# Strassen's scheme for seven of nine channel groups of a fused attention, expert and FFN kernel

## The chip, the cores and the metric

One core of a Trainium2 chip runs the whole program. The metric is device time in microseconds (us) of one launch; lower is better. Engines: TensorE (PE; its weight loads are listed as PEld), VectorE (DVE), ScalarE (ACT), GpSimd (POOL) and SyncE (SP), whose queue issues most DMAs.

## The reference

```python
attn = softmax(q @ mean_pool8(k).T / 8) @ mean_pool8(v)      # 8 x 8 heads, 576 tokens, 64 wide
x = attn as [4608 tokens, 512]
e = argmax of 8 gate logits (or the previous token's expert, if a local gate says so)
x = softmax(logits)[e] * (relu(x @ w1[e]) @ w2[e])           # 512 -> 1024 -> 512
xn = (x - mean) / sqrt(var + 1e-6) * g_ln
out = x + relu(xn @ w_ch1) @ w_ch2                           # 512 -> 2048 -> 512
```

The change is in the last line, the channel FFN. All data are float32; the kernel makes each float32 product from float16 halves: `hi*hi + hi*lo + lo*hi`, three matmuls that add up in one PSUM bank.

## The kernel before

There are three stages, and every engine follows an order written out by hand.

The attention stage works on 36 tiles of 128 tokens. Routing then sorts the tokens by expert into 39 blocks of 128 rows (`NF = 39`).

The expert stage is the loop `for k in range(NF + 1)`. Block `k` takes 48 matmuls with 512 columns (`moe1`, `moe2`, two halves of 12 each). When the expert changes, new weights are loaded into `f1` and `f2` and split into float16 halves in `s1` and `s2` (`splits1`, `splits2`, line 540). The channel weights come in as 64-bit words and are converted by `conv_slot` and `conv_b2` in the same loop.

The channel FFN works on 9 groups of 512 tokens. `ln(j)` normalises a tile, splits it and has a DMA transpose (line 945, on SP's queue) write it to `xnT`. A *unit* is one of 16 slices of 128 hidden channels of one group: `ffn1(u)` is 12 matmuls of 512 columns into one bank of `ps_f`, ScalarE and VectorE take ReLU and both halves out of it (lines 968 and 969), and `ffn2(u)`, two units later (`LAG`), is 12 matmuls into the four banks of `ps_a`, which hold the group's 512 tokens over 16 units. `ffn2_out` adds the residual, and GpSimd scatters the rows to `out` (line 986).

`mix(k, n)` puts units into the expert loop at `RATE = 1.15` a block from block `FIRST = 8` on; the rest follow when the loop is over, and `ffn2_last` orders the last seven so that tiles finish one after the other. All of PSUM is in use: two banks each for `ps_m` and `ps_f`, four for `ps_a`.

`hs`, `xn` and the like are float32 work tiles; `tick` moves generators (`chains`) on by small steps, so that the small vector work of one tile lies between the matmuls of others.

## Time and profile before

| | |
|---|---|
| median of 3 runs | 1373.8 us (1373.62 to 1373.91) |
| the profiled execution: its own time | 1379.85 us |
| its span on the core | 1377.9 us, mean granted clock 0.986 |
| attention, routing and the first expert blocks | 0 to about 291 us |
| experts with channel units between them | 291 to 811 us |
| channel units alone | 811 to 1371 us |

The rows below are of the profiled execution. A matmul's listed time contains the pipeline behind it, so the time that one takes in a stream is read from the starts of two groups. A bracket at the end of a row is the idle time of the engine before it, and what ended that.

### The profile page before, as it was taken

What the parts mean: (1) busy time and instruction counts of PE and PEld (TensorE: products, weight loads), DVE (VectorE), ACT (ScalarE), POOL (GpSimd) and SP (SyncE); (2) the same over time, 40 slices, a digit from 0 to 9 for tenths busy, and PEclk for the clock granted to TensorE, in tenths of its full rate; (3) what the DMA queues carried; (4) which work ended last, traced back from release to release, by engine and by line L of the source; (5) the groups of instructions that cost most, each with busy time, mean ns of one, the idle gap of its engine ahead of it and who ended that gap; (6) DMA issues with size and microseconds to landing.
All of it is one profiled execution on the core that took longest, in us unless ns stands there. A gap on an engine that the chain in (4) does not pass through costs nothing. (4 is left out here: it accounts for less than half of the span.)

```text
span 1377.9 us, 20409 instructions
## 1 busy us (share of the span) xinstructions
PE 1319.3 (96%) x6512; PEld 662.7 (48%) x6512; DVE 555.0 (40%) x1387; ACT 447.7 (32%) x943; POOL 329.0 (24%) x374
## 2 busy tenths in 40 slices
PE   6999789789999999999999999999999999999998
PEld 5999534334444444444444434444444444444443
DVE  7777884555664243343254531221212222122211
ACT  5888424444443232333143431121211212121110
POOL 3667253343332112321111220110201101020101
PEclk9999989999999999999999999999999999999999
DMA  9997377887995575676476750120201102021000
GB/s 306 296 298 238 138 236 160 146 179 181 216 212 111 93 147 147 132 150 156 90 190 154 190 153 0 39 54 9 68 17 54 39 31 54 8 70 23 31 0 31
DMA packets 213274, 166.85 MB, mean 121 GB/s; under 512 B 163550, under 2 KB 171998, under 8 KB 213152
## 3 DMA queue, kind: packets, MB, share of 16 engines
q1 hardware_dynamic: 199424, 119.32, 36.0%
q0 software_dynamic: 9120, 29.30, 6.9%
q10 hardware_dynamic: 4608, 16.78, 4.9%
q8 instruction: 54, 0.88, 0.3%
q14 instruction: 68, 0.56, 0.2%
HBM read 216.30 MB, written 29.28 MB: 178 GB/s over the span
## 5 line engine op out<-in xcount | busy, mean ns | idle before, releaser
L959 PE MATMUL f_ps<-xnT,c_sb 128*128 128x512 f16 x1728 | 395.6, 379 | 0.0
L978 PE MATMUL a<-c_sb,hf 128*128 128x512 f16 x1680 | 385.6, 379 | 0.0
L969 DVE SCALAR_TENSOR_TENSOR hf<-f_ps,hf 128x512 f16<-128x512 f32 x140 | 96.6, 690 | 436.1 <-ACT hf L968 418.4
L959 PEld LDWEIGHTS <-c_sb 128*128 128x128 f16 x1728 | 169.1, 98 | 203.9
L978 PEld LDWEIGHTS <-hf 128*128 128x128 f16 x1680 | 164.4, 98 | 198.2
L623 PE MATMUL y_ps<-s,hT 128*128 128x512 f16 x936 | 220.4, 386 | 14.7 <-DMA hT<-hs 11.8
L610 PE MATMUL h_ps<-s,xT 128*128 128x512 f16 x936 | 216.9, 382 | 8.5 <-DVE hs L615 6.9
L968 ACT ACTIVATE hf<-f_ps 128x512 f16<-128x512 f32 x140 | 83.4, 596 | 412.6 <-PE f_ps L959 412.6
L623 PEld LDWEIGHTS <-hT 128*128 128x128 f16 x936 | 92.5, 99 | 130.3 <-DMA hT<-hs 13.8
L610 PEld LDWEIGHTS <-xT 128*128 128x128 f16 x936 | 92.2, 98 | 120.7 <-issue 12.8
L986 POOL DMA_INDIRECT out_dram<-yt,ti x36 | 35.4, 984 | 355.9 <-DVE yt L985 312.5
L614 ACT ACTIVATE hs<-h_ps 128x512 f16<-128x512 f32 x78 | 46.5, 597 | 224.7 <-PE h_ps L610 205.9
L615 DVE SCALAR_TENSOR_TENSOR hs<-h_ps,hs 128x512 f16<-128x512 f32 x78 | 53.8, 690 | 160.0 <-ACT hs L614 116.5
L631 POOL DMA_INDIRECT y_d<-yr,sidx x39 | 41.5, 1064 | 213.2 <-ACTq L1067 92.6
L540 DVE SCALAR_TENSOR_TENSOR s<-f,s 128x1024 f16<-128x1024 f32 x53 | 63.8, 1242 | 19.4 <-ACT s L535 18.5
L303 ACT ACTIVATE p<-s,nm 128x72 f32<-128x72 f32 x288 | 65.8, 338 | 8.1 <-DVE nm L289 7.9
L931 POOL TENSOR_TENSOR rs<-rs,mhalf 128x1 f32<-128x1 f32 x36 | 20.8, 577 | 179.3 <-DVE rs L930 179.3
L942 POOL TENSOR_TENSOR xns<-xn,xns 128x512 f16<-128x512 f32 x36 | 42.2, 1173 | 89.1 <-issue 42.4
L279 PE MATMUL s<-kb,qt 128*128 128x144 f32 (+1 forms) x320 | 45.4, 297 | 14.0 <-ACT kb L203 13.6
L535 ACT ACTIVATE s<-f 128x1024 f16<-128x1024 f32 x56 | 55.7, 1047 | 0.0
L337 PE MATMUL o<-v,pt 128*128 128x148 f32 (+1 forms) x320 | 51.8, 298 | 3.5 <-DVE r L356 3.1
L940 ACT ACTIVATE xn<-yt,rs 128x512 f32<-128x512 f32 x36 | 29.3, 814 | 79.3 <-DVE rs L934 72.7
(198 smaller groups left out, 1032.9 us busy)
## 6 DMA issues: line engine op xcount, KB each, us to landing
f<-in_w_dram SPq DMA_DIRECT2D x288, 512.0 KB
xrow_d<-xr SPq DMA_DIRECT2D x36, 260.5 KB
yt<-y_d SPq DMA_DIRECT2D x36, 256.5 KB
kt<-in_kT_dram SPq DMA_DIRECT2D x16, 576.0 KB
qt<-in_qT_dram SPq DMA_DIRECT2D x18, 512.0 KB
vt<-in_vP_dram SPq DMA_DIRECT2D x16, 512.0 KB
c_sb<-in_c_dram ACTq DMA_DIRECT2D x16, 512.0 KB
shared<-in_c_dram ACTq DMA_DIRECT2D x8, 512.0 KB
```

The lines of the kernel that those rows point to most:

```text
L303: nc.scalar.activation(out=p32[:, h, :], in_=s[:, h // 4, NK * (h % 4):NK * (h % 4) + NK], func=AF.Exp, bias=nm[:, h:h + 1],)
L337: nc.tensor.matmul(out=o[c][lo:hi, 2 * VC * e:2 * VC * (e + 1)], lhsT=pt[:, 2 * c + e, lo:hi], rhs=vb[:, 4 * c + 2 * e:4 * c + 2 * e + 2, ...
L535: A.activation(out=hi, in_=src, func=AF.Copy, scale=SW)
L540: V.scalar_tensor_tensor(out=lo[:, 0:v], in0=src[:, 0:v], scalar=SW, in1=hi[:, 0:v], op0=ALU.mult, op1=ALU.subtract)
L610: nc.tensor.matmul(out=ps, lhsT=xT[:, x, c], rhs=s1[:, w, c, 512 * half:512 * half + 512], start=(n == 0), stop=(n == 11))
L614: A.activation(out=hs[:, 0], in_=ps, func=AF.Relu)
L615: V.scalar_tensor_tensor(out=hs[:, 1], in0=ps, scalar=0.0, in1=hs[:, 0], op0=ALU.max, op1=ALU.subtract)
L623: nc.tensor.matmul(out=ps, lhsT=hT[:, f // 4, x, f % 4], rhs=s2[:, w, f], start=(f == 0 and x + w == 0), stop=(f == 7 and x == 1),)
L959: nc.tensor.matmul(out=ps, lhsT=c1_sb[:, w, c, 128 * f:128 * f + 128], rhs=xT[:, x, c], start=(n == 0), stop=(n == 11))
L968: A.activation(out=hf[:, 0], in_=ps, func=AF.Relu)
L969: V.scalar_tensor_tensor(out=hf[:, 1], in0=ps, scalar=0.0, in1=hf[:, 0], op0=ALU.max, op1=ALU.subtract)
L978: nc.tensor.matmul(out=acc_t[t], lhsT=hf_t[u][:, x, 128 * t:128 * t + 128], rhs=c2_sb[:, w, f], start=(f == 0 and n == 0), stop=(f == NC2 ...
```

## The change

The first two groups (`NPL = 2`, 32 units) stay as they were, but at `RATE = 0.87` and with the last five held back (`HOLD`) until the expert loop is over. The other seven groups use the Winograd form of Strassen's scheme: tokens, model width and hidden width are halved, and seven products of half-size blocks take the place of eight, in both layers. The matmuls of these groups have 256 columns instead of 512. For one group, layer 1 is 8 steps (`l1_step`) of 7 products of 6 matmuls; layer 2 is 112 pieces (2 token halves, 8 slices, 7 products) of 3 matmuls, which `fill` puts between and behind them.

The scheme's 15 sums of each layer: four of the inputs, per group (`prep`, both halves of each tile pair written to `xs`, then `xpose` has four DMA transposes of 128 x 1792 float16 write `xnT`); four of the weights, once (`sums_of`, in the expert loop after the conversions, three steps at each `mix`; they go to DRAM and come back by `load_comb` into the buffers of the expert weights and into places of the channel weights that are no longer used); seven of the products (in `l1_step` between PSUM and float32 tiles for layer 1; in `evac` for layer 2). The seven hidden combinations are split again into halves (`post_a`, `post_b`, `post_c`).

```diff
--- before.py
+++ after.py
...
-SX, SW, SN, SC1, SC2 = 2.0 ** 7, 2.0 ** 5, 2.0 ** 3, 2.0 ** 4, 2.0 ** 5
+SX, SW, SN, SC1, SC2 = 2.0 ** 7, 2.0 ** 5, 2.0, 2.0 ** 4, 2.0 ** 5
...
+    c1c_d = dram.tile([4, 128, 2, 2, DC // 2], F16, name="c1c_d")
+    c2c_d = dram.tile([4, 128, 2, NCV // 2, DM // 2], F16, name="c2c_d")
...
-    LASTU = 7
-    hf2 = [None]
-    RATE = 1.15
+    RATE = 0.87
...
+    def ftile(u):
+        return (u % NC2 + (NC2 // 2 if u // NC2 == NPL - 1 else 0)) % NC2
+
     def ffn1(u):
-        g, f = divmod(u, DC // 128)
+        g, f = u // NC2, ftile(u)
         assert all(4 * (f // 4) + i in done for i in range(4))
...
+    NPL = 2
+    NU = NPL * NC2
+    HOLD = 5
...
-                load_f1(k, c, 512 * half)
+                if k < NF - 1:
+                    load_f1(k, c, 512 * half)
...
+    hole1 = c1_sb[:, :, 0:2, DC // 2:DC]
+    hole2 = c2_sb[:, :, NC2 // 2:NC2, DM // 2:DM]
...
+    S_w = [hole1, w1c(f1h, 0), w1c(f1h, 1), w1c(f2h, 0)]
+    T_w = [hole2, w2c(f2h, 1), w2c(s1h, 0), w2c(s1h, 1)]
+
+    def load_comb(t, d, i):
+        for x in range(2):
+            nc.sync.dma_start(out=t[:, x], in_=d[i, :, x])
...
+    def sums_of(q, h):
+        tA, tB = shared[:, 0:512].bitcast(F32), shared[:, 512:1024].bitcast(F32)
+        outs = [cw2[:, 0:512].bitcast(F16), cw2[:, 512:1024].bitcast(F16), ct2.bitcast(F16)]
...
+        def out(t):
+            o = outs[n[0] % 3].rearrange("p (x f) -> p x f", x=2)
+            A.copy(out=o[:, 0], in_=t)
+            yield 0
+            G.tensor_tensor(out=o[:, 1], in0=t, in1=o[:, 0], op=ALU.subtract)
+            i = n[0]
+            n[0] += 1
+            for _ in range(2):
+                yield 0
+            src = o if q == 0 else o.rearrange("p x (c d) -> p x c d", c=2)
+            nc.sync.dma_start(out=dst[i], in_=src)
...
+            tt(ta, a21[:, 0], a22[:, 0], ALU.add)
+            yield 0
+            tt(tb, a21[:, 1], a22[:, 1], ALU.add)
+            yield 0
+            tt(ta, ta, tb, ALU.add)
+            yield from out(tA)
+            tt(tb, ta, a11[:, 0], ALU.subtract)
+            yield 0
+            tt(tb, tb, a11[:, 1], ALU.subtract)
...
+    SUMS = 3
...
-        if k >= FIRST and nu[0] < min(int(RATE * (k - FIRST) + n), NC2 * groups[0]):
+        if k >= FIRST and nu[0] < min(int(RATE * (k - FIRST) + n), NC2 * groups[0], NU - HOLD):
...
+        for _ in range(SUMS):
+            if ncv[0] > len(jobs):
+                next(sums, None)
...
+    def xpose(g):
+        for s in range(2):
+            xs = xs_t.pop((g, s))
+            for x in range(2):
+                nc.sync.dma_start_transpose(out=xnT[:, x, :, 128 * s:128 * s + 128], in_=xs[:, x].rearrange("p o t -> p (o t)"))
...
+        T1, T2, T3, T4 = (tmpT[:, n] for n in range(4))
+        xs = pl_t["pp"].tile([128, 2, 7, HW_], F16, tag="xs", name="xs")
+        xs_t[g, s] = xs
+        a12 = yl[0][:, 0:DM].rearrange("p (n t) -> p n t", n=2)
+        V.tensor_tensor(out=T1, in0=b1, in1=a1, op=ALU.subtract)
+        nc.gpsimd.tensor_tensor(out=T3, in0=b2, in1=b1, op=ALU.subtract)
+        V.tensor_tensor(out=T2, in0=b2, in1=T1, op=ALU.subtract)
+        V.tensor_tensor(out=T4, in0=a2, in1=T2, op=ALU.subtract)
+        A.copy(out=xs[:, 0, 0:2], in_=a12)
+        A.copy(out=xs[:, 0, 2], in_=b2)
+        yield 0
+        A.copy(out=xs[:, 0, 3:7], in_=tmpT)
+        V.tensor_tensor(out=xs[:, 1, 0:2], in0=a12, in1=xs[:, 0, 0:2], op=ALU.subtract)
+        V.tensor_tensor(out=xs[:, 1, 2], in0=b2, in1=xs[:, 0, 2], op=ALU.subtract)
+        if g > NPL:
+            yl_load(g + s, 1 - s)
+        nc.gpsimd.tensor_tensor(out=xs[:, 1, 3:7], in0=tmpT, in1=xs[:, 0, 3:7], op=ALU.subtract)
...
+        if k == NF - 1:
+            for _ in sums:
+                pass
+            load_comb(S_w[1], c1c_d, 1)
+            load_comb(S_w[2], c1c_d, 2)
...
-    while nu[0] < NU:
-        if nu[0] % 2:
-            norm_next(NB)
-        else:
-            load_next(NB + 2)
+    mo.close()
+    pp = pl_t["pp"] = ctx.enter_context(tc.tile_pool(name="pp", bufs=2, side="right", reuse_waits="tile"))
+    load_comb(S_w[0], c1c_d, 0)
+    load_comb(T_w[2], c2c_d, 2)
+    load_comb(T_w[3], c2c_d, 3)
+    load_comb(T_w[0], c2c_d, 0)
+
+    run(lumps, 1)
+    while nu[0] < NU + LAG:
         unit()
         tick(99)
-    ffn2_last()
+        if lumps:
+            run(lumps, 2)
+            if not lumps:
+                xpose(NPL)
+    stats_in(bsel.rearrange("p a b -> p (a b)"))
+    tis = [[take(bsel.rearrange("p a b -> p (a b)"), 1).bitcast(U32) for _ in range(2)] for _ in range(2)]
+    yl_load(NPL + 1, 0)
+    yl_load(NPL + 1, 1)
+    while outq:
+        outq.pop(0)()
...
+    def l1(ps, lhs, i, op, first):
+        n = 0
+        for w, x in TERMS:
+            for k in range(2):
+                nc.tensor.matmul(
+                    out=ps, lhsT=lhs(w, k, i), rhs=xnT[:, x, 2 * op + k], start=(first and n == 0), stop=(n == 5), skip_group_check=True,
+                )
+                n += 1
...
+    L2 = (
+        (0, 0, 0, raw2(NI, 0)), (1, 0, 1, raw2(0, 0)), (4, 1, 0, com2(1)), (5, 1, 1, com2(2)),
+        (3, 2, 0, com2(0)), (6, 2, 1, raw2(0, 1)), (2, 3, 0, com2(3)),
+    )
...
+                        for m, (x, w) in enumerate(TERMS):
+                            nc.tensor.matmul(
+                                out=l2["acc"][b][:, HW_ * o:HW_ * o + HW_], lhsT=h[:, x, op], rhs=rhs(w, i),
+                                start=(i == 0 and o == 0 and m == 0), stop=(i == NI - 1 and m == 2), skip_group_check=True,
+                            )
...
+        A.activation(out=t, in_=P1, func=AF.Copy, scale=SC)
+        yield add(a1, P1, a1)
+        yield add(a1, P2, a1)
+        yield add(U2, P6, t)
+        yield add(U3, P7, U2)
+        yield add(b2, P5, b2)
+        G.tensor_tensor(out=b2, in0=b2, in1=U3, op=ALU.add)
+        yield add(t, P5, U2)
+        yield add(a2, P3, a2)
+        G.tensor_tensor(out=a2, in0=a2, in1=t, op=ALU.add)
+        yield add(b1, P4, b1)
+        G.tensor_tensor(out=b1, in0=b1, in1=U3, op=ALU.add)
...
+        V.tensor_tensor(out=st[:, 0], in0=c22, in1=raw[:, 2], op=ALU.add)
+        V.tensor_tensor(out=st[:, 1], in0=raw[:, 0], in1=st[:, 0], op=ALU.subtract)
+        V.tensor_tensor(out=st[:, 3], in0=raw[:, 1], in1=st[:, 1], op=ALU.add)
...
+    def post_c(fast=False):
+        if pend[0] is None:
+            return
+        raw, st = pend[0][0], pend[0][2]
+        for s in range(2):
+            hi(s, 3, 4, st)
+            if fast and s == 0:
+                low(V, 0, 3, 4, st)
+        for s in range(2):
+            low(V, s, 0, 3, raw)
+        for s in range(fast, 2):
+            low(nc.gpsimd, s, 3, 4, st)
+        pend[0] = None
+
...
+        l1(a, A11, i, 0, True)
+        post_a()
+        A.copy(out=s1, in_=a)
+        run(eq, 3)
+        l1(b, A12, i, 1, True)
+        post_b()
+        l1(c, S1, i, 3, True)
+        V.tensor_tensor(out=raw[:, 1], in0=b, in1=s1, op=ALU.add)
+        l1(a, S2, i, 4, False)
+        A.copy(out=U2, in_=a)
+        run(eq, 3)
+        post_c()
+        if outq:
+            outq.pop(0)()
+        fill(gaps[0])
+        l1(a, S3, i, 5, False)
+        A.copy(out=U3, in_=a)
+        V.tensor_tensor(out=c22, in0=c, in1=U3, op=ALU.add)
+        fill(gaps[1])
+        run(eq, 3)
+        l1(a, A22, i, 6, False)
+        A.activation(out=raw[:, 0], in_=a, func=AF.Relu)
+        run(lumps, 2 if g == NPL else 1)
+        fill(gaps[2])
+        l1(c, S4, i, 2, False)
+        V.tensor_tensor(out=raw[:, 2], in0=c, in1=U2, op=ALU.add)
+        A.activation(out=raw[:, 1:3], in_=raw[:, 1:3], func=AF.Relu)
+        V.tensor_scalar(out=c22, in0=c22, scalar1=0.0, scalar2=None, op0=ALU.max)
+        V.tensor_tensor(out=st[:, 2], in0=c22, in1=raw[:, 0], op=ALU.subtract)
+        run(eq, 2)
+        pend[0] = (raw, c22, st, [], (g, i))
...
+    for g in range(NPL, NG):
+        last = g + 1 == NG
+        for i in range(NI):
+            n = g > NPL or i > 1
+            l1_step(g, i, ((4, 3, 0) if i < NI - 1 else (2, 1, 0)) if n else (0, 0, 0))
+        post_a()
+        post_b()
+        post_c(True)
+        run(lumps, -1)
+        if not last:
+            xpose(g + 1)
+        if g + 2 < NG:
+            lumps += [prep(g + 2, 0), prep(g + 2, 1)]
+        fill(4)
+        for n in range(8 if not last else 10):
+            fill(7)
+            run(eq, -1)
+            if n in (2, 4):
+                outq.pop(0)()
+            if n > 1 and g + 2 < NG:
+                run(lumps, 1)
...
```

## Rows read from the trace of the kernel before

**Rows 1.** The page: busy time of each engine; a group (count, busy, mean ns).

```profile
PE 1319.3 (96%) x6512; PEld 662.7 (48%) x6512; DVE 555.0 (40%) x1387; ACT 447.7 (32%) x943; POOL 329.0 (24%) x374
...
L969 DVE SCALAR_TENSOR_TENSOR hf<-f_ps,hf 128x512 f16<-128x512 f32 x140 | 96.6, 690 | 436.1 <-ACT hf L968 418.4
```

**Rows 2.** Windows: us, busy (instructions) of PE, PEld, DVE, ACT, POOL, clock, DMA.

```profile
300.00:400.00 100.00, 96.57 (x448) 43.59 (x446) 64.18 (x132) 47.56 (x77) 35.51 (x38) 1.00 0.87 203
...
801.00:811.60 10.60, 7.69 (x27) 2.90 (x26) 5.33 (x7) 3.82 (x5) 4.78 (x4) 0.84 0.85 239
...
1100.00:1200.00 100.00, 100.00 (x465) 45.37 (x464) 21.53 (x48) 17.08 (x27) 10.84 (x12) 1.00 0.12 32
```

**Rows 3.** Timeline of TensorE, FFN alone: start us, us, engine, line, shapes.

```profile
1055.08 2.75 PE L959 MATMUL f_ps<-xnT,c_sb 128*128 128x512 f16 x12
...
1060.26 2.75 PE L959 MATMUL f_ps<-xnT,c_sb 128*128 128x512 f16 x12
```

**Rows 4.** Timeline of TensorE, routing: narrower matmuls with weights of their own.

```profile
158.62 0.28 PE L681 MATMUL cps<-oh,shared 128*128 128x288 f16 x1 [0.55 <-DVE oh L675]
...
158.75 0.28 PE L682 MATMUL cps<-oh,shared 128*128 128x288 f16 x1
...
158.87 0.38 PE L153 MATMUL tps<-c_sb,shared 128*128 128x512 f16 x1
...
168.37 5.77 PEld L752 LDWEIGHTS <-c_sb 128*128 128x128 f16 x36 [1.68 <-DVE c_sb L743]
```

**Rows 5.** Windows of line 959: busy (count) up to 811.4 us.

```profile
0.00:811.40 811.40, 101.70 (x444) 43.44 (x444) 0.98 0.73 182
```

**Rows 6.** Timeline of TensorE at the end of the expert stage.

```profile
806.30 0.38 PE L623 MATMUL y_ps<-s,hT 128*128 128x512 f16 x1 [1.86 <-ACT s L535]
...
807.57 4.22 PE L623 MATMUL y_ps<-s,hT 128*128 128x512 f16 x11 [0.88 <-DVE s L540]
```

**Rows 7.** Timeline of the conversion stage: the longer wait of TensorE.

```profile
396.02 2.75 PE L610 MATMUL h_ps<-s,xT 128*128 128x512 f16 x12 [1.81 <-DVE hs L615]
```

**Rows 8.** Groups, 300 to 400 us: count, busy us, mean ns, idle before.

```profile
L133 POOL TENSOR_TENSOR c_sb<-ct,c_sb 128x512 f16<-128x512 f32 x9 | 10.5, 1164 | 19.6 <-ACTq L1078 13.2 <-ACT c_sb L132 4.4 <-ACTq L1067 1.9
...
L582 DVE SCALAR_TENSOR_TENSOR xs<-xg,xs 128x512 f16<-128x512 f32 x6 | 7.8, 1301 | 9.2 <-ACT xs L581 7.8 <-DMA hT<-hs 1.4
```

**Rows 9.** The same groups, 500 to 600 us.

```profile
L582 DVE SCALAR_TENSOR_TENSOR xs<-xg,xs 128x512 f16<-128x512 f32 x7 | 4.8, 691 | 7.2 <-ACT xs L581 7.0 <-DVEq L1067 0.3
```

**Rows 10.** Timeline: single instructions of VectorE, ScalarE and GpSimd.

```profile
163.06 0.46 DVE L727 TENSOR_TENSOR c_sb<-c_sb,oh 128x288 f32<-128x288 f32 x1
...
159.62 0.40 ACT L687 COPY tot<-cps 128x288 f32<-128x288 f32 x1 [5.13 <-DVE shared L686]
...
1057.79 1.16 POOL L942 TENSOR_TENSOR xns<-xn,xns 128x512 f16<-128x512 f32 x1 [2.12 <-issue]
...
1057.87 0.60 ACT L968 ACTIVATE hf<-f_ps 128x512 f16<-128x512 f32 x1 [0.21 <-PE f_ps L959]
```

**Rows 11.** Timeline: VectorE and GpSimd at the same time, routing.

```profile
168.48 2.14 POOL L544 TENSOR_TENSOR s<-ptmp,s 128x512 f16<-128x512 f32 x1 [2.23 <-ACT s L535]
...
169.51 1.13 DVE L746 TENSOR_TENSOR bend<-c_sb 128x8 f32<-128x8 f32 x1
```

**Rows 12.** Timeline: one DMA transpose issued with all queues empty.

```profile
1255.79 1.23 SPq L945 DMA_TRANSPOSE xnT<-xns  x1
```

**Rows 13.** Windows: us, clock, DMA share, GB/s: that transpose, then weight loads.

```profile
1257.25:1257.50 0.25, 1.00 1.13 218
...
1258.25:1258.50 0.25, 1.00 0.11 19
...
198.00:198.25 0.25, 1.00 1.07 393
```

**Rows 14.** Timeline of the last output: matmul, evacuation, scatter.

```profile
1368.47 2.75 PE L978 MATMUL a<-c_sb,hT 128*128 128x512 f16 x12
...
1373.79 0.97 POOL L986 DMA_INDIRECT out_dram<-yt,ti  x1 [5.13 <-issue]
```

More of the change, by code (lines that the diff above doesn't have):

```diff
@@ L25 @@
 DC = 4 * DM
+NCV = DC // 128
 NT = T // 128
@@ L979, in ffn2_mm @@
                 out=acc_t[t], lhsT=hf_t[u][:, x, 128 * t:128 * t + 128], rhs=c2_sb[:, w, f],
-                start=(f == 0 and n == 0), stop=(f == NC2 - 1 and n == 2),
+                start=(n0 == 0 and n == 0), stop=(n0 == NC2 - 1 and n == 2),
             )
@@ L1086, in tile_attention_moe_ffn, with all_sums @@
+    def all_sums():
+        for r in range(2):
+            for c in range(2):
+                yield from sums_of(0, (r, c))
+        for h in range(4):
+            yield from sums_of(1, h)
+    sums = all_sums()
+    SUMS = 3
     pexp(0)
@@ L1109, in mix, with stats_in @@
             conv_b2()
+        for _ in range(SUMS):
+            if ncv[0] > len(jobs):
+                next(sums, None)
+    NG = NT // 4
+    NI = NC2 // 2
+    HW_ = DM // 2
+    xnT = s2f[:, 0:7168].rearrange("p (x o t) -> p x o t", x=2, t=256)
+    snap = s2f[:, 7168:8192].bitcast(F32).rearrange("p (n t) -> p n t", n=2)
+    tmpT = shared.bitcast(F32).rearrange("p (n t) -> p n t", n=4)
+    stat = {}
+    def stats_in(buf):
+        used[0] = 0
+        stat.update(half=take(buf, 1), st=take(buf, 2, 6), mv=take(buf, 2, 2), rs=take(buf, 2, 2))
+        V.memset(stat["half"], -0.5)
@@ L1111, in tile_attention_moe_ffn, with run @@
+    lumps, eq = [], []
+    def run(q, n):
+        while q and n:
+            if next(q[0], None) is None:
+                q.pop(0)
+            else:
+                n -= 1
+    PRE = NF - 5
+    pre = []
     AHEAD = 4
@@ L1170, in tile_attention_moe_ffn @@
             load_next(k)
+        if not pre and nl[0] == 4 * NPL and stored[0] >= 4 and k >= last_block(4 * NPL + 3) + 2:
+            yl_load(NPL, 0)
+            yl_load(NPL, 1)
+            pre.append(k)
+        elif pre and k >= PRE:
+            if k == PRE:
+                stats_in(wq.tile([128, DM], F32, tag="xn", name="xn"))
+                lumps.extend((prep(NPL, 0), prep(NPL, 1)))
+            for _ in range(2):
+                if len(pre) <= 8:
+                    next(lumps[len(pre) > 4])
+                    pre.append(k)
         if k == FIRST - 1:
@@ new lines, in tile_attention_moe_ffn, with fill, evac, add @@
+    l2g = l2_steps()
+    def fill(n):
+        for _ in range(n):
+            if next(l2g, None) is None:
+                return
+    def evac(acc, yr, ti):
+        G = nc.gpsimd
+        P1, P2, P6, P7, P5, P3, P4 = (acc[b][:, HW_ * o:HW_ * o + HW_] for _, b, o, _ in L2)
+        ya, yb = yr
+        t = tq.tile([128, HW_], F32, tag="et", name="et")
+        U2 = tq.tile([128, HW_], F32, tag="eu2", name="eu2")
+        U3 = tq.tile([128, HW_], F32, tag="eu3", name="eu3")
+        def add(out, p, x):
+            return V.scalar_tensor_tensor(out=out, in0=p, scalar=SC, in1=x, op0=ALU.mult, op1=ALU.add)
+        a1, a2, b1, b2 = (y[:, HW_ * d:HW_ * d + HW_] for y in yr for d in range(2))
+        A.activation(out=t, in_=P1, func=AF.Copy, scale=SC)
[10 more added lines that the diff above has]
+        G.tensor_tensor(out=b1, in0=b1, in1=U3, op=ALU.add)
+        for n in range(2):
+            V.tensor_copy(out=ti[n], in_=yr[n][:, DM:YROW])
+        outq.extend(lambda n=n: G.indirect_dma_start(
+            out=out, out_offset=bass.IndirectOffsetOnAxis(ap=ti[n], axis=0), in_=yr[n][:, 0:DM], in_offset=None,
+        ) for n in range(2))
+        yield 0
@@ new lines, in l1_step @@
+    def l1_step(g, i, gaps):
+        a, b, c = bank(), bank(), bank()
+        raw = tq.tile([128, 3, 256], F32, tag="raw", name="raw", bufs=2)
+        c22 = tq.tile([128, 256], F32, tag="c22", name="c22")
+        st = tq.tile([128, 4, 256], F32, tag="st", name="st")
+        U2 = tq.tile([128, 256], F32, tag="u2", name="u2", bufs=2)
+        s1, U3 = snap[:, 0], snap[:, 1]
+        l1(a, A11, i, 0, True)
[29 more added lines that the diff above has]
+        pend[0] = (raw, c22, st, [], (g, i))
@@ new lines, in tile_attention_moe_ffn @@
+    lumps += [prep(NPL + 1, 0), prep(NPL + 1, 1)]
+    for g in range(NPL, NG):
+        last = g + 1 == NG
+        for i in range(NI):
+            n = g > NPL or i > 1
[16 more added lines that the diff above has]
+                run(lumps, 1)
@@ L1185, in words @@
+    run(eq, -1)
+    while outq:
+        outq.pop(0)()
 def words(w):
```

201 lines of the change are left out of this document (168 added, 33 removed).

## The prediction

> **What bounds the kernel now.** I read the page first, then windows by stage, then TensorE's timeline. On the page TensorE is busy in 96% of the span, no other engine in more than 40% [rows 1]. A busy TensorE need not be a full one, so the windows come next: where only channel units run, the granted clock is 1.00, its upper level of 2.4 GHz, and VectorE and ScalarE are busy in a fifth of the time [rows 2]. The timeline there shows that TensorE streams without a hole: a unit's 24 matmuls of 512 columns start 5.18 us after those of the unit before, 215.8 ns each, where 512 columns at 2.4 GHz are 213.3 ns, so some 2.5 ns lie between two [rows 3]. The channel FFN is 144 units, 746 us of the 1378; 37 of them lie in the expert loop (444 matmuls of line 959 by 12) [rows 5]. TensorE sets the time, through the number of columns that it streams, and the change cuts just that.
>
> **The matmuls.** A group before is 16 units x 24 = 384 matmuls of 512 columns, 82.9 us. After it is 8 x 42 + 112 x 3 = 672 of 256 columns. What does one of 256 columns take, each with 128 columns of weights of its own? The stage with 512 cannot show whether the weight load still hides. The nearest rows are two matmuls of 288 columns with different weights: they start 0.13 us apart, and the next follows 0.12 us later; 288 columns are 120 ns [rows 4]. So the load hides at 120 ns. I take 106.7 + 2.5 = 109.2 ns: 672 x 109.2 = 73.4 us, 9.5 us less a group, **66.5 us** for seven. The lower bound of the gap is nothing (71.7 us a group, 78 us gained in all). The other bound is the run of 86 columns, where 36 weight loads take 5.77 us, 162 ns each [rows 4]; there both operands step over 36 elements, here every run is contiguous, so I stand by the 288-column row.
> The Trainium skill speaks against this: "TensorE: Matmul & The Clock Gate", section "Back-to-back issue gap", gives 81 ns for a matmul of 128 columns in a stream with weight loads where the columns alone take 56. By that surcharge of 25 ns, 672 x 7 matmuls would lose 118 us and the change would end slower, at 1458. The 288-column rows show no such surcharge.
>
> **What the expert loop gains and loses.** Ten units fewer run in it; their work comes later or shrinks, and that is in the sum above. Added are the weight sums: 8 calls of 9 VectorE additions of 512 columns (0.69 us, as line 582 takes when GpSimd leaves it alone [rows 9]), 4 ScalarE copies (0.60) and 4 GpSimd subtractions (1.16) [rows 10], spread at three steps a `mix`, twelve of 136 steps a block, from about block 17 to 28. That is 4.4 us of VectorE and 3.3 us of GpSimd a block of some 15 us. The conversions that end there cost as much per block: between 300 and 400 us VectorE was busy 64%, GpSimd 36% [rows 2], nine of GpSimd's subtractions among it [rows 8], and TensorE lost two waits on VectorE, the longer 1.8 us [rows 7]. So **+3 us**, between 0 and 10. SP's queue gets 32 stores that wait for GpSimd's subtraction, and behind them stand the transposes of `hs`; issued two steps after the subtraction, they should find it done.
> At the end of the loop the profile loses about 4.5 us to the last expert's weight splits: 1.86 and 0.88 us of waits [rows 6], and a lower clock (0.84 in these 10.6 us [rows 2]), under which 11 matmuls took 4.22 us instead of 2.5. After the change no unit covers the last two blocks, since the 27 allowed units are used up at block 37; but the normalisations, on which VectorE waited there, are gone too. **0**, from -5 to +5. `load_comb` puts 2 MB on SP's queue in front of the last block's transposes and 6 MB in all behind it; at 393 GB/s [rows 13] 2 MB take 5.3 us, the last six MB some 16 us, under 31 us of plain units (60 + 84 matmuls). `xpose` for the first Strassen group stands behind them.
>
> **The transposes.** Before, 128 x 1024 is issued in 1.23 us [rows 12]; its data move at about 210 GB/s and are through 2.5 us after the start of the issue [rows 13], 1.3 of these moving. Now four of 128 x 1792 can start only when a group's layer 1 has read `xnT`, and the next group's layer 1 needs them all. By size each takes 1.3 x 1.75 = 2.3 us, four with the first's 1.2 us of issue 10.4 us. The cover is 60 pieces of layer 2, 60 x 3 x 109.2 ns = 19.7 us. Cost 0; at half that rate it would still be 19.6 us.
>
> **Entering the Strassen stage.** In the first two steps of the first group there is no layer 2 to fill in. The products share one bank, and each must be read before the next adds to it: TensorE's result reaches ScalarE 0.2 us after its last column (12 matmuls from 1055.08 on stream until 1057.67 [rows 3], ScalarE starts at 1057.87 [rows 10]), a copy of 256 columns takes about 0.37 us (0.40 for 288 [rows 10]). Two or three such gaps a step are some 1.5 us, 3 us for two steps; the first work tiles lie where the old outputs are still being scattered, another 3. **+6 us**, 3 to 12.
>
> **The steady steps.** A step is 42 + 21 matmuls, 6.9 us. VectorE's part: seven operations of 256 columns (0.43 us, between 0.46 for 288 [rows 10] and 0.69 for 512), two of 384 (0.56), one maximum: 4.5 us. GpSimd: two subtractions of 512 columns, 2.3 us. ScalarE: five reads of 0.37 to 0.60 and four copies, 4.3 us. Each fits alone. But VectorE and GpSimd block each other: at 168.48 a GpSimd subtraction that alone takes 1.16 takes 2.14 us beside VectorE, and the tiny VectorE operation after it 1.13 us, to the moment GpSimd ends [rows 11]; line 582, with two inputs in SBUF, took 1301 ns beside the conversions [rows 8] and 691 later [rows 9]. Operations with one input in PSUM show little of the kind: line 969 has a mean of 690 ns over all 140 [rows 1].
> Counted by group, within the eight steps (492 matmuls, 53.7 us): VectorE's operations with both inputs in SBUF are 8 x 2.84 + 2.4 for a `prep` = 25.1 us, GpSimd's 18.6 + 2.9 + 1.9 for an `evac` = 23.4. Together 48.5 us of 53.7, and in a plain step they take turns: VectorE until about 4.2 us into the step, GpSimd from there to 6.5. It fits, with little room. Where `prep` subtracts 1024 columns on GpSimd (2.3 us), VectorE comes late to `c22`, which TensorE needs before the last product; about 1 us of slack is there. I take 1.5 us a group, **+10.5 us**; the bounds are 0 and, if the two engines never overlapped at all (44.2 + 23.4 = 67.6 us), 13.9 x 7 = 97 us.
> The Trainium skill says the same of this pair: "SBUF — State Buffer", "Who interferes with whom": an operation with two SBUF inputs and a GpSimd one that reads SBUF exclude each other for a whole instruction. By that rule the 48.5 us hold; it is the rule that speaks against this change.
>
> **The end of each group.** After the last product the chain is: 0.2, add 0.43, ReLU of 512 columns 0.60, three additions 1.3, copy 0.60, subtractions 0.69 and 0.56, with some 0.3 us of hand-overs and the second ReLU's two operations beside it about 5.0 us, until layer 2 may use the eighth slice. Eleven pieces and two matmuls stand before, 3.8 us. TensorE waits 1.2 us, and about 0.5 us more where the second token half takes over the banks that `evac` still reads: 1.7 x 7 = **+12 us**, 0 to 25.
>
> **The last output.** Now the last stream ends at 1371.06, and the span 6.85 us later, with the scatter issued at 1373.79 [rows 14]. After: three VectorE additions follow the last product, a GpSimd addition (about 0.6), and two scatters, issued one after the other (0.97 us). **+1.5 us**, 0 to 4.
>
> **Sum.** -66.5 + 3 + 0 + 6 + 10.5 + 12 + 1.5 = -33.5 us. The profiled execution took 1379.85 us, 6.05 above the median of the runs; 1379.85 - 33.5 - 6.05 = **1340 us** as a median. With the bounds of the small terms the likeliest case lies between 1320 and 1362.
>
> **The rivals.** *The vector pair sets the step* (the other side). Place: the eight steps of each group, TensorE waiting for the reads of `c22` and `raw`. Against it the 48.5 of 53.7 us; for it the two engines' blocking, and that in-order queues put PSUM reads behind a blocked operation. Without its 10.5 us the sum is -44; so from 44 / 56 = 0.79 us a step on the kernel is slower than before. At the full bound, 1340 + 86 = 1426 us. Chance 0.16, of which 0.03 end within 0.2% and 0.01 below.
> *All is covered.* The end-of-group waits and the steps cost nothing, as TensorE's queue and `fill` hide them: 1340 - 22 = 1318 us, down to 1310 if the entrance is cheap too. Chance 0.14.
> *The transposes come late.* The rows show one alone; if four land 25 us after their start, six groups wait 4 us: 1364 us. Against it the doubled cover. Chance 0.05.
> *Narrow matmuls don't hide their weights*, 162 ns as in the strided run: 672 x 162 = 108.9 us a group, +26: 1340 + 66.5 + 182 = 1589 us. Chance 0.03.
>
> **How the numbers follow.** The forecast has 0.62. Faster by over 0.2% (2.7 us, about what a measurement here can tell): 0.62 + 0.14 + 0.05 + 0.01 = 0.82; within it 0.03; slower 0.12 + 0.03 = 0.15. The range from 1312 to 1372 holds the forecast, the late transposes and most of the covered case, and leaves out the slower ones.
>
> **What would show it.** In the changed profile: matmuls of 256 columns 109 ns apart in the runs of layer 2 after a group's steps; a Strassen group of 76 to 78 us from layer 1 to layer 1, against 73.4; in the steps, waits of TensorE on `c22` and on the snapshots of tens of us in total; one wait on the halves of `h` per group, of about a microsecond; none on `xnT`. I am wrong if the distance of two matmuls in a free run is over 120 ns, if VectorE's and GpSimd's operations stretch until a step takes 7.7 us or more, or if the expert loop gets longer by more than the ten units taken out account for.

## The result and the profile after

The changed kernel takes **1386.95 us** (median of 4 runs, 1385.77 to 1388.08); the kernel before took 1373.71 us beside it (1372.45 to 1373.91). The ratio is 1.0098, 95% interval 1.0081 to 1.0116: slower by 1%, where 1340 us were forecast.

The profiled execution took 1388.08 us, 8.2 more than that of before. The page after, the line of TensorE and of the group that gained most idle time (the last two numbers are the idle time before its instructions, and what ended most of it):

```profile
PE 1268.1 (91%) x8528; PEld 859.2 (62%) x8528; DVE 851.8 (61%) x2028; ACT 629.3 (45%) x1395; POOL 533.2 (38%) x539
...
L616 PE MATMUL h_ps<-s,xT 128*128 128x512 f16 x936 | 224.7, 392 | 32.2 <-DVE hs L621 30.4
```

TensorE's busy time fell by 51 us against [rows 1], and the span grew by 8.4, so it has holes now. It waits 30.4 us for `hs` (the first-layer result of an expert half, which must leave its PSUM bank before the next half may use it). In the kernel before it was 6.9, as the same group of its page shows:

```profile
L610 PE MATMUL h_ps<-s,xT 128*128 128x512 f16 x936 | 216.9, 382 | 8.5 <-DVE hs L615 6.9
```

Where the holes lie is read from windows of the expert loop. Two of the kernel before, columns as in [rows 2]:

```profile
400.00:450.00 50.00, 50.00 (x234) 22.62 (x232) 21.32 (x46) 16.84 (x30) 13.57 (x15) 1.00 0.68 132
500.00:550.00 50.00, 50.00 (x233) 22.69 (x232) 20.98 (x42) 16.06 (x26) 9.15 (x11) 1.00 0.68 167
```

and the same two of the changed kernel, with the one that follows:

```profile
400.00:450.00 50.00, 45.73 (x205) 20.16 (x204) 22.24 (x47) 17.07 (x31) 13.59 (x15) 0.97 0.78 129
500.00:550.00 50.00, 43.95 (x188) 19.14 (x187) 30.75 (x53) 16.25 (x28) 15.93 (x16) 0.93 0.68 178
550.00:600.00 50.00, 46.90 (x218) 21.12 (x216) 26.36 (x51) 16.51 (x30) 17.62 (x19) 1.00 0.55 133
```

Before, TensorE ran 233 matmuls of 512 columns in 50 us, which is full. After, it runs 205 in the last stretch of the conversions, and 188 and 218 where the weight sums run. Counted over all such windows the conversion stage (291 to 450 us) lost 68 matmuls and the sums' stage (500 to 650) 73, each of 215.8 ns: 14.7 and 15.8 us. Neither VectorE (61% busy), nor ScalarE and GpSimd (a third each) are near their limit there. Over the whole loop TensorE's listed waits come to 33.1 us, against 9.9 in the kernel before.

The holes are therefore a matter of order, and the timeline shows it. Changed kernel, conversion stage:

```profile
318.21 2.75 PE L629 MATMUL y_ps<-s,hT 128*128 128x512 f16 x12
...
318.56 1.57 DVE L588 SCALAR_TENSOR_TENSOR xs<-xg,xs 128x512 f16<-128x512 f32 x1 [2.85 <-ACT xs L587]
...
321.30 0.69 DVE L130 SCALAR_TENSOR_TENSOR ct<-shared,ct 128x512 uint32<-128x512 uint32 x1
322.02 0.63 ACT L134 ACTIVATE ct<-ct 128x512 f32<-128x512 f32 x1 [3.50 <-DVE ct L130]
322.68 0.62 ACT L135 CAST c_sb<-ct 128x512 f16<-128x512 f32 x1
...
323.47 0.60 ACT L620 ACTIVATE hs<-h_ps 128x512 f16<-128x512 f32 x1 [0.17 <-ACTq L1075]
...
324.10 0.69 DVE L621 SCALAR_TENSOR_TENSOR hs<-h_ps,hs 128x512 f16<-128x512 f32 x1 [2.11 <-ACT hs L620]
...
324.84 4.38 PE L616 MATMUL h_ps<-s,xT 128*128 128x512 f16 x12 [3.88 <-DVE hs L621]
```

The half was ready in PSUM before 318.5 us (TensorE went on to other matmuls at 318.21). ScalarE idled 3.50 us at the head of its queue, at line 134, for VectorE's conversion; `hs` stood behind it, though nothing kept it from running. At the rate of 0.87 no channel unit lies between these two halves, so TensorE stood still for 3.88 us. Then it paid a second time, as windows of the same stretch show (the number behind the five busy times is the granted clock):

```profile
324.80:327.20 2.40, 2.36 (x8) 0.94 (x8) 1.06 (x4) 0.00 (x0) 0.89 (x1) 0.71 0.56 124
327.20:329.20 2.00, 2.00 (x6) 0.76 (x5) 1.30 (x4) 0.00 (x0) 0.58 (x1) 0.50 1.14 314
```

After the stop the granted clock fell to its lower level of 1.2 GHz, and 12 matmuls took 4.38 us instead of the 2.75 of [rows 3].

In the sums' stage the head of ScalarE's queue is a copy of a weight sum (line 1129), here once behind VectorE's addition, once behind the store of its buffer three sums back:

```profile
506.93 0.62 ACT L1129 CAST ct<-shared 128x512 f16<-128x512 f32 x1 [1.81 <-DVE shared L1140]
...
509.11 4.33 PE L616 MATMUL h_ps<-s,xT 128*128 128x512 f16 x12 [2.94 <-DVE hs L621]
...
523.75 2.75 PE L629 MATMUL y_ps<-s,hT 128*128 128x512 f16 x12
524.88 0.62 ACT L1129 CAST cw<-shared 128x512 f16<-128x512 f32 x1 [4.82 <-DMA c1c_d<-cw]
525.41 2.00 ACT L541 ACTIVATE s<-f 128x1024 f16<-128x1024 f32 x2
...
527.31 0.58 ACT L620 ACTIVATE hs<-h_ps 128x512 f16<-128x512 f32 x1
...
529.61 1.78 PE L616 MATMUL h_ps<-s,xT 128*128 128x512 f16 x6 [3.11 <-DVE hs L621]
```

The second time line 1129 waited 4.82 us for the store, the weight splits of the next expert (line 541) queued behind it, and `hs` behind those. From 460 to 790 us ScalarE waited in this line 36.9 us for additions (14 times) and 14.5 us for stores (3 times).

The Strassen stage, first one and the same point of two groups, then the start of a stretch in which nothing is waited for:

```profile
1040.92 0.61 PE L1463 MATMUL p<-c_sb,h 128*128 128x256 f16 x4 [1.55 <-DVE h L1526]
...
1119.00 0.61 PE L1463 MATMUL p<-c_sb,h 128*128 128x256 f16 x4 [1.55 <-DVE h L1526]
...
1358.40 0.49 PE L1463 MATMUL p<-s,h 128*128 128x256 f16 x3
```

From 1358.40 us to the last three, which start at 1372.16 (below), 126 matmuls of 256 columns take 13.76 us, 109.2 ns each. A steady group takes 1119.00 - 1040.92 = 78.08 us, 4.7 more than its stream. From 900 to 1300 us the main waits are these (total, times, longest), each five times in five groups:

```profile
PE p L1463 <- DVE h L1526: 7.8, 5, 1.6
PE l_ps L1422 <- ACT s L1562: 3.3, 5, 0.7
PE l_ps L1422 <- DVE c L1577: 3.1, 5, 0.6
PE l_ps L1422 <- ACT s L1576: 1.8, 5, 0.4
```

Read from one start to the next, the holes of a group are 1.72 us at the halves of `h`, 2.15 at the three others together, 0.33 where the second token half takes over a bank, and 0.5 in smaller ones.

The last output, which answers to [rows 14]:

```profile
1360.59 0.96 POOL L1506 DMA_INDIRECT out_dram<-yr,bsel  x1 [2.53 <-DMA out_dram<-yr,bsel]
...
1372.16 0.49 PE L1463 MATMUL p<-s,h 128*128 128x256 f16 x3
...
1375.92 0.98 POOL L1506 DMA_INDIRECT out_dram<-yr,bsel  x1 [0.16 <-POOL yr L1503]
1382.07 0.97 POOL L1506 DMA_INDIRECT out_dram<-yr,bsel  x1 [5.16 <-issue]
```

The two scatters don't go out one after the other in 0.97 us: 5.16 us lie between them, in which the second waits for the first to land. Its own row names no releaser; the second of the pair before, at 1360.59, names the first one's DMA. From the last matmul to the end are 13.8 us, against 6.85 before.

The account by spans: matmuls -66.5; expert loop +29.0 (the plain units alone start at 788.79 us, where 811.62 less ten units of 5.18 would be 759.8); Strassen stage beyond its stream 552.6 - 513.8 = +38.8; last output +6.95. Together +8.3, measured +8.4.

### The profile page after: what moved, and what is told of

The parts are those of the page before. It is cut to its first block, busy times and chain, and to the rows that moved or that the text cites. A ratio compares the mean times of both kernels' runs of the same rounds, so it can differ in the third digit from the quotient of the medians.

```text
span 1386.3 us, 26188 instructions
## 1 busy us (share of the span) xinstructions
PE 1268.1 (91%) x8528; PEld 859.2 (62%) x8528; DVE 851.8 (61%) x2028; ACT 629.3 (45%) x1395; POOL 533.2 (38%) x539
## 3 DMA queue, kind: packets, MB, share of 16 engines
q8 instruction: 70, 1.15, 0.3%
## 5 line engine op out<-in xcount | busy, mean ns | idle before, releaser
L1463 PEld LDWEIGHTS <-h 128*128 128x128 f16 x2352 | 229.4, 98 | 42.1 <-DVE h L1526 12.8
L616 PE MATMUL h_ps<-s,xT 128*128 128x512 f16 x936 | 224.7, 392 | 32.2 <-DVE hs L621 30.4
L1526 POOL TENSOR_TENSOR h<-st,h 128x512 f16<-128x512 f32 x105 | 128.9, 1246 | 215.2 <-ACT h L1522 160.5
L1463 PE MATMUL p<-c_sb,h 128*128 128x256 f16 x1344 | 184.5, 273 | 12.1 <-DVE h L1526 10.9
L1422 PE MATMUL l_ps<-s,c_sb 128*128 128x256 f16 x1344 | 165.0, 272 | 4.8 <-ACT s L1576 3.8
L1422 PE MATMUL l_ps<-s,f 128*128 128x256 f16 x1008 | 137.4, 272 | 13.3 <-ACT s L1562 8.4
L1422 PEld LDWEIGHTS <-f 128*128 128x128 f16 x1008 | 98.5, 98 | 28.6 <-issue 17.3
L1463 PE MATMUL p<-s,h 128*128 128x256 f16 x672 | 110.0, 273 | 0.0
L966 PE MATMUL f_ps<-xnT,c_sb 128*128 128x512 f16 x384 | 87.9, 379 | 0.0
L979 PE MATMUL a<-c_sb,hf 128*128 128x512 f16 x384 | 87.8, 379 | 0.0
L1526 DVE TENSOR_TENSOR h<-raw,h 128x384 f16<-128x384 f32 x112 | 66.9, 638 | 0.0
```

The costliest lines, as they stand in the source:

```text
L616: nc.tensor.matmul(out=ps, lhsT=xT[:, x, c], rhs=s1[:, w, c, 512 * half:512 * half + 512], start=(n == 0), stop=(n == 11))
L966: nc.tensor.matmul(out=ps, lhsT=c1_sb[:, w, c, 128 * f:128 * f + 128], rhs=xT[:, x, c], start=(n == 0), stop=(n == 11))
L979: nc.tensor.matmul(out=acc_t[t], lhsT=hf_t[u][:, x, 128 * t:128 * t + 128], rhs=c2_sb[:, w, f], start=(n0 == 0 and n == 0), stop=(n0 == NC ...
L1422: nc.tensor.matmul(out=ps, lhsT=lhs(w, k, i), rhs=xnT[:, x, 2 * op + k], start=(first and n == 0), stop=(n == 5), skip_group_check=True,)
L1463: nc.tensor.matmul(out=l2["acc"][b][:, HW_ * o:HW_ * o + HW_], lhsT=h[:, x, op], rhs=rhs(w, i), start=(i == 0 and o == 0 and m == 0), stop ...
L1526: e.tensor_tensor(out=h[:, 1, lo:lo + n], in0=src[:, :, 128 * s:128 * s + 128], in1=h[:, 0, lo:lo + n], op=ALU.subtract)
```

## The experiments

Twelve kernels ran, in four sets; each ratio is to runs of the kernel before on the same chip (medians of 1374 to 1377 us there). Each set has theories of its own, named with it.

**First set: is it the units that left, or the sums that came?** Theory A says the loop lost its cover as ten units went; B, that the sums hold it up. The kernel before with its rate of units lowered:

```
-    RATE = 1.15
+    RATE = 0.87
```

> The kernel before with one number changed: RATE 0.87 instead of 1.15, no sums, no Strassen. Theory A (fewer channel units between the expert blocks leave TensorE without cover while VectorE and ScalarE work down their queues, sums or no sums): the expert loop loses what the changed kernel lost there, 25 to 30 us, so about 1400 us. Theory B (the weight sums on VectorE and GpSimd cost the time, the rate only lets the conversion stage suffer): 10 to 15 us, about 1386 us.

Measured 1387.01 us, ratio 1.0072 (1.0044 to 1.0100): +10 us, as B had it. The kernel before with `sums_of`, `all_sums` and the calls in `mix` added, and nothing that reads the sums:

> The kernel before at its RATE of 1.15 with the weight sums and their stores to DRAM added in the expert loop as the change has them; nothing reads them. Theory A: the sums hide, 0 to 4 us, at most 1378 us. Theory B: 12 to 17 us, 1386 to 1391 us.

Measured 1405.35 us, 1.0193 (1.0151 to 1.0234). Both theories had it too low: the sums alone, at the full rate of units, cost 26 to 28 us, and nearly all of it where they run: 135 matmuls fewer than in the kernel before from 500 to 650 us, 29 us. Its first window there:

```profile
500.00:550.00 50.00, 42.89 (x186) 18.67 (x185) 29.97 (x49) 15.48 (x26) 15.47 (x15) 0.93 0.62 159
```

The changed kernel with the rate raised to 1.15:

> The changed kernel with RATE 1.15 instead of 0.87; its 27 units then run out near block 31. Theory A: most of the 29 us of the expert loop come back, about 1362 us (1358 to 1370). Theory B: only the part before the sums comes back, 12 us, about 1375 us.

Measured 1382.96 us, 1.0051 (1.0019 to 1.0082), about 6 us better than the change, where theory A had 25 and B 12: the conversion stage was as full as in the kernel before (264, 216 and 233 matmuls in its windows from 291 us on, against 264, 216 and 234), the sums' stage was not (187 from 500 to 550), and the units were used up early, so that from 700 to 800 us it lost 106 matmuls. So both are at work; which part is the larger the third set shows. From 500 to 650 us the sums lost 57 matmuls here and 135 in the run before, at the same rate: their price depends on what else the queues hold, and what made this difference was not tested.

**Second set: what of the sums?** Theory Q is the order of ScalarE's queue, theory L the lock between VectorE and GpSimd. Fewer steps at a time:

```
-    SUMS = 3
+    SUMS = 2
```

> The changed kernel with two steps of the weight sums at each of the four places of a block instead of three, so that the 136 steps end about 5.7 blocks later. Theory Q (queue order): the loss of the stage with sums comes from copies of the sums that stand at the head of ScalarE's in-order queue, in front of the evacuation of an expert half, while their last addition is not done or the store of their buffer, three sums back, has not landed (two waits for a store of together 10.0 us and one of 4.5 us in the trace of the changed kernel). With 8 us between sums instead of 5.5 us the waits for stores go: TensorE's waits for the halves of h fall from 30.4 us to about 24, and the time by 6 to 9 us, to about 1379. Theory L (lock): the loss comes from VectorE's additions of two SBUF inputs that exclude GpSimd's subtractions; as many of them collide, so 1385 to 1388.

Measured 1397.35 us, 1.0177 (1.0119 to 1.0235): worse than the change. Both theories missed. The stage became longer and lost as much in each stretch (205 matmuls from 550 to 600, 199 from 700 to 750); TensorE waited 34.2 us for `hs`. The copies still waited for stores, up to 7.1 us, and for additions. I read this as a price that goes by how many expert halves have a copy in front of them, not by the number of sums in a block; no run counts it.

A copy later behind its addition:

```
+            for _ in range(2):
+                yield 0
             A.copy(out=o[:, 0], in_=t)
```

> The changed kernel with two more steps between the last addition of a weight sum and its copy on ScalarE, three steps at each place as before; a sum then takes 6.25 steps, which is the density of the run with two steps at each place. Theory Q: the copy finds its addition done, and the evacuation behind it waits for no sum: beside what two steps per place give, the waits for additions go too, about 12 to 15 us below the changed kernel, 1372 to 1375. Theory L: no better than the run with two steps per place, 1379 to 1387.

Measured 1391.9 us, 1.0115 (1.0045 to 1.0185). That is not to be told from the change. The later copies waited no less: 27.2 us for additions and 26.3 us for stores. The low halves on VectorE:

```
-            G.tensor_tensor(out=o[:, 1], in0=t, in1=o[:, 0], op=ALU.subtract)
+            V.tensor_tensor(out=o[:, 1], in0=t, in1=o[:, 0], op=ALU.subtract)
```

> The changed kernel with the low halves of the weight sums subtracted by VectorE instead of GpSimd (32 instructions of 0.69 us more on VectorE, 32 of 1.16 us fewer on GpSimd). Theory L: without GpSimd's subtraction beside them the additions all take 0.69 us, and the loss of the stage with sums falls by half: about 1379. Theory Q: VectorE's queue is 22 us fuller, and the evacuations stand behind that as well: 1387 to 1395.

Measured 1389.8 us, 1.0105 (1.0066 to 1.0145), again not to be told from the change. The additions did run unhindered (duration min, median, max):

```profile
L1140 DVE TENSOR_TENSOR shared<-shared,c_sb x40: 673/689/694, 446.3 to 629.5; 128x512 f32<-128x512 f32 x40
```

In the changed kernel the longest of these took 1.60 us. Yet nothing was won. The lock is that VectorE and GpSimd keep each other waiting, as in [rows 11]; without it in the additions the loop lost as much. The run alone leaves open whether the 22 us of subtractions that VectorE took over ate what the lock gave back; the run with all of it on GpSimd, below, answers that.

The fourth kernel of the set edits the Strassen stage:

```
-        for s in range(fast, 2):
-            low(nc.gpsimd, s, 3, 4, st)
...
-                out=l2["acc"][b][:, HW_ * o:HW_ * o + HW_], lhsT=h[:, x, op], rhs=rhs(w, i),
+                out=l2["acc"][b][:, HW_ * o:HW_ * o + HW_], lhsT=h[:, x if op < 3 else 0, op], rhs=rhs(w, i),
...
+                order = [(i, n) for i in range(NI) for n in (0, 1, 2, 4, 5)] + [(i, n) for i in range(NI) for n in (3, 6)]
```

> Two edits of stages that don't touch one another, read from the windows. First: the low halves of the four summed operands of h (GpSimd, two instructions of 2.58 us a step) are left out, and the products read the high half in their place, with as many matmuls as before. Theory L: VectorE's three waits of a step fall, and a steady group from 78.08 us to about 75.5, all seven about 17 us. Theory Q: 78.1 as before. Second, last output: the last accumulation makes all products of the first tile (five of seven per channel block) before the remaining two, and adds and scatters that tile while these run; the second scatter then no longer waits for the landing of the first. From the last matmul to the end of the span: 13.8 us to about 7. In all 1363 by L, 1380 by Q.

The `low` that `post_c(True)` gives VectorE at a group's end went too, and the last output's additions on GpSimd moved to VectorE (`evac_end`). Measured 1359.95 us, 0.9891 (0.9834 to 0.9949). By the trace the Strassen stage took 534.5 us instead of 552.6, -18.1: in the steady groups the waits on `h` and on line 1562's snapshot are gone, those on `c22` and on the other snapshot are not. The 17 us of theory L are there, but the run cannot say how much of it is the lock, since the halves left out were also the work that TensorE waited for at the end of each group. That the lock acts in this stage too is seen in this run where GpSimd's long subtraction is left:

```profile
1009.49 2.40 POOL L1285 TENSOR_TENSOR xs<-shared,xs 128x1024 f16<-128x1024 f32 x1 [13.26 <-ACT xs L1280]
...
1009.97 2.20 DVE L1559 TENSOR_TENSOR st<-c,raw 128x256 f32<-128x256 f32 x1
```

An addition that takes 0.42 us elsewhere in this run took 2.20, and ended 0.3 us after GpSimd's subtraction. "SBUF — State Buffer", "Who interferes with whom", of the Trainium skill says just this of two SBUF inputs beside a GpSimd operation that reads SBUF; the rows agree. And the last output:

```profile
1343.67 4.75 PE L1465 MATMUL p<-s,h 128*128 128x256 f16 x42 [0.19 <-DVE eu L1523]
...
1345.14 0.96 POOL L1526 DMA_INDIRECT out_dram<-yr,bsel  x1 [8.49 <-DVE yr L1537]
...
1351.55 0.97 POOL L1526 DMA_INDIRECT out_dram<-yr,bsel  x1 [5.45 <-issue]
```

The first tile's scatter goes out under the last 42 matmuls, and the span ends at 1355.8, 7.5 us after the last of them instead of 13.8. This bears out the waiting of the second scatter for the first: it now lies mostly under matmuls and additions, and the second goes 1.7 us after its data are ready.

**Third set: take the sums out of ScalarE's way.** Theory S blames the stores, A the wait for additions, Q again ScalarE's queue as a whole. Only the stores moved, to GpSimd's own queue right behind its subtraction:

```
-            nc.sync.dma_start(out=dst[i], in_=src)
+            nc.gpsimd.dma_start(out=dst[i], in_=src)
```

> The changed kernel with the stores of the weight sums issued by GpSimd right behind its subtraction instead of by SyncE two steps later. Theory S (stores): a store stands in SyncE's queue and rings behind loads of expert weights and transposes, so that ScalarE's copy into its buffer three sums later waits for it (4.5 to 5.1 us, three times) with the evacuation of an expert half behind it; these waits go, TensorE's waits for halves of h in the stage with sums fall from 11.0 us to about 6, and the time by about 6 us, to 1381. Theory A (additions): the copies wait for VectorE's additions, that stand behind other work there; unchanged, 1385 to 1389.

Measured 1390.39 us, 1.0103 (1.0058 to 1.0148): no gain. Two waits for stores were left, shorter than before, and those for additions stayed:

```profile
ACT cw L1129 <- DVE shared L1140: 21.2, 9, 4.5
ACT ct L1129 <- DVE shared L1140: 17.2, 6, 5.5
...
ACT cw L1129 <- DMA c2c_d<-cw: 4.1, 1, 4.1
ACT cw L1129 <- DMA c1c_d<-cw: 3.5, 1, 3.5
```

Copy, subtraction and store together on GpSimd, one step behind the last addition, so that ScalarE holds nothing of the sums, at two steps a place:

```
-            A.copy(out=o[:, 0], in_=t)
+            G.tensor_copy(out=o[:, 0], in_=t)
...
-    SUMS = 3
+    SUMS = 2
```

> The changed kernel with copy, subtraction and store of each weight sum on GpSimd, one step behind the last addition, two steps at each place (the density of the run with two steps at each place, 1397). ScalarE then holds nothing of the sums; VectorE's additions stay. Theory Q (ScalarE's queue): the evacuations of expert halves wait for no sum any more; the stage with sums loses at most 4 us of 20, about 1378. Theory A (VectorE's additions, and what excludes them beside GpSimd, now 32 copies more): the loss stays or grows, 1395 to 1405.

Measured 1379.23 us, 1.0006 (0.9974 to 1.0038), 1.7 points below the run with the same two steps and ScalarE's copies. VectorE does as many additions, GpSimd more work than ever, and in four of the five windows from 450 to 700 us TensorE is full or nearly so (228 to 234 matmuls). The first row here is one of them, the second is the fifth window:

```profile
500.00:550.00 50.00, 50.00 (x233) 22.68 (x232) 31.72 (x54) 13.69 (x23) 26.51 (x30) 1.00 0.75 189
...
650.00:700.00 50.00, 46.64 (x210) 20.72 (x208) 31.06 (x53) 17.98 (x27) 26.96 (x31) 0.97 0.73 181
```

In these five windows it runs 1138 matmuls; the kernel before runs 1166, the run with two steps and ScalarE's copies 1075. That decides between the theories: most of the price is the place in ScalarE's queue, not the work, since fewer steps alone and the stores' move alone had won nothing. The longest wait that is left, 3.4 us, comes from VectorE's queue, like the one of the fastest run below. Without the sums' arithmetic at all (`out` and `tt` gone, a block of the weights stored in the place of each sum):

> The changed kernel without the arithmetic of the weight sums: parts of the weights as they are are stored in their place, through SyncE as before; the rest is unchanged, so the products are of the wrong operands. If the sums' arithmetic is what the stage with sums loses, TensorE has as many matmuls there as in the kernel before (233 per 50 us), and the time falls by 15 to 17 us, to about 1371; what is left of the loss is then the conversion stage at the lower rate of units, 13 us. If their stores are what costs, 1382 to 1387.

An earlier form of this kernel, in the first set, gave no time. Measured 1368.52 us, 0.9953 (0.9922 to 0.9985), 18 to 20 us below the change. The sums' stage is full, the conversion stage is not:

```profile
400.00:450.00 50.00, 46.17 (x207) 20.50 (x206) 19.68 (x45) 15.19 (x27) 13.56 (x16) 0.97 0.74 133
500.00:550.00 50.00, 50.00 (x233) 22.72 (x232) 16.25 (x35) 14.27 (x23) 6.54 (x9) 1.00 0.75 186
```

So the conversions' loss belongs to the rate of units and the other to the sums. Then all mends at once:

```
-    NPL = 2
+    NPL = 3
-    RATE = 0.87
+    RATE = 1.3
```

with the sums on GpSimd, the new order of the last output, and two conditions for the third group's tiles adapted (`stored[0] >= 4 * NPL - 4`, and the first `prep` started when its tiles are loaded).

> Three plain groups and six by Strassen's scheme, 1.3 units per block in the expert loop; the sums' copies and subtractions on GpSimd as above, two steps at each place; the last accumulation makes the products of its first tile first, as in the run without low halves. By the terms measured so far against the kernel before: matmuls -57, entrance and steps +12 and +28, last output 0, expert loop 0 (if neither the rate of units nor the sums cost anything here) to +26 (if the sums cost what they cost in the kernel before alone): 1357 to 1383. Theory Q 1358 to 1364, theory A 1375 to 1385.

Measured **1356.56 us**, 0.9844 (0.9797 to 0.9891): faster than both kernels, and just under the range of theory Q. The conversion stage is as full as in the kernel before, the sums' stage nearly so but for one long wait, which the second window holds:

```profile
400.00:450.00 50.00, 50.00 (x234) 22.66 (x232) 22.59 (x47) 17.42 (x31) 13.59 (x15) 1.00 0.67 133
500.00:550.00 50.00, 43.59 (x193) 19.24 (x192) 31.97 (x61) 17.05 (x26) 23.14 (x25) 0.93 0.83 194
```

The timeline of this run shows what that wait is due to:

```profile
531.84 0.58 ACT L620 ACTIVATE hs<-h_ps 128x512 f16<-128x512 f32 x1
...
535.28 0.69 DVE L1140 TENSOR_TENSOR shared<-shared 128x512 f32<-128x512 f32 x1
...
535.89 2.35 DVE L546 SCALAR_TENSOR_TENSOR s<-f,s 128x1024 f16<-128x1024 f32 x2
...
538.16 0.69 DVE L621 SCALAR_TENSOR_TENSOR hs<-h_ps,hs 128x512 f16<-128x512 f32 x1
538.90 4.70 PE L616 MATMUL h_ps<-s,xT 128*128 128x512 f16 x12 [5.24 <-DVE hs L621]
```

ScalarE took its half of `hs` in time, at 531.84. VectorE, which takes the other half, came to it only at 538.16: from 533.67 on three additions of the sums and two weight splits (line 546) stood in front of it in its queue. It is the same fault on the other engine.

**Last run: the same with the sums as in the change** (ScalarE, SyncE, three steps):

> The run with three plain groups, 1.3 units per block and the changed last output, but with the weight sums as in the change: copies on ScalarE, stores on SyncE, three steps at each place. Theory Q: full rate of units doesn't cover the copies that stand in front of the expert halves (in the kernel before with the sums alone they cost 28 us at 1.15 units per block); the time is 15 to 25 us above the 1356.6 of the run with the sums on GpSimd, 1372 to 1382. Theory R (the rate of units alone is what matters): within 4 us of it, 1353 to 1361.

Measured 1372.08 us, 0.9963 (0.9927 to 1.0000), 16 us above the run before it. From 500 to 550 us TensorE ran 161 matmuls at a clock of 0.87. The rate of units does not cover the copies; the order of ScalarE's queue has to be right as well. (Stores and steps differ too between these two runs; on their own they had won nothing.)

## Why the prediction was wrong

**The matmuls: right.** 109.2 ns each in a free run, as taken from the 288-column row; -66.5 us. The Trainium skill's surcharge ("TensorE: Matmul & The Clock Gate", "Back-to-back issue gap", 81 ns for 128 columns) does not show at 256 columns either.

**The transposes, the loads of the sums, the end of the loop: right at 0.** TensorE waits for no `xnT` in the steady groups, and the 144 matmuls of the plain units after the loop take 819.87 - 788.79 = 31.1 us, which is 144 x 215.8 ns. The end of the loop loses what it lost before, by other waits: 31 matmuls in its last 48.8 us, against 28 in the last 61.6.

**The expert loop: this step failed**, +3 forecast, +29.0 measured, 26 of the 47 us between forecast and median. It stood on two sentences. "The conversions that end there cost as much per block ... and TensorE lost two waits" took the price of the sums from the busy shares of a stage with other work. The engines did have the time; but the sums put a ScalarE instruction, which depends on VectorE and on a store, in front of an evacuation that depends on neither. The run with ScalarE free of them takes most of that loss away with the same additions, and the run without the sums' arithmetic is 18 to 20 us faster than the change. The second sentence counted the ten units that leave as matmuls only. They were also the cover between two expert halves: with 0.87 units a block the same waits behind conversions, which 1.15 units hid, come through, +10 us in the kernel before and 14.7 by the windows after. And neither allowed for the lower clock behind a long stop: five groups of 12 matmuls in these two stages took 4.3 to 4.4 us. The third sign of being wrong that the prediction named, a loop that gets longer than the ten units account for, is the one that came. None of the rivals held it: the chance of a slower kernel, 0.15, stood on the vector pair and on the weight loads.

**The steps and ends of the groups, the entrance: mechanism right, size short.** 28.5 us forecast, 38.8 measured. A steady group takes 4.7 us over its stream instead of 3.2: its end 2.05 (1.7 forecast), its steps 2.7 (1.5 forecast). The first group, from 819.87 to 900.98 us with 630 matmuls, takes 12.3 over its stream, against 6 + 3.2; the last, where less is waited for, 3.2. The rival on the other side, the vector pair that sets the step, came in part only. By the starts of the steps most of the eight in a steady group take 6.9 to 7.1 us, but the third and fourth, in which `evac` or `prep` runs beside them, take 7.65 and 7.70, just the 7.7 named as a sign. On average a step loses 0.34 us; 0.79 would have been needed to make the kernel slower by this alone.

**The last output: mis-sized**, +1.5 forecast, +6.95 measured. I took the second scatter as issued behind the first; it waits for the first to land. [rows 14] already had a sign of it, 5.13 us of idle time before the last scatter of the kernel before. Its data were ready earlier:

```profile
1371.26 0.69 DVE L985 SCALAR_TENSOR_TENSOR yt<-a,yt 128x512 f32<-128x512 f32 x1 [3.84 <-PE a L978]
```

From 1371.95 to 1373.79 us it waited for something other than its data; the landing of the scatter before it fits.

**The median:** the profile of before lay 6.05 us above its median, that of after 1.1; the 4.9 us between them are the rest of the miss (26 + 10.3 + 5.5 + 4.9 = 46.7).

What stays open: how much of the 18 us that the low halves cost in the Strassen stage is the lock, and how much the length of the chain at a group's end; why the sums cost 135 matmuls in one kernel and 57 in another at the same rate of units; and why the scatter at the very end takes 5.16 us to land where others take 2.53.

## What to carry to other kernels

When work is added to engines that have time, don't price it by busy shares: ask for each added instruction what it waits for, and what stands behind it in its engine's in-order queue. Put it on an engine whose queue holds nothing that the bottleneck needs, even if it runs longer there; the additions that stayed on VectorE still held up one evacuation in the fastest run. And work that is taken out of the bottleneck's stage may have been the cover of waits that were there all along; look for the waits that it hid before it is moved.
